# Swapping neighbours in a hand-held order table: four score or value products, two copies and two normalizations in the front of an attention and gated-convolution kernel

## The chip, the cores and the metric

The kernel runs on one core of one Trainium2 chip. The metric is device time in microseconds (us); lower is better.

## The reference

```python
# q, k, v: (8 batches, 12 heads, 448 positions, 64)
scores = scale * np.matmul(q, k.transpose(0, 1, 3, 2))
m = np.max(scores, axis=-1, keepdims=True)
e = np.exp(scores - m)
attn = e / (np.sum(e, axis=-1, keepdims=True) + np.exp(-m) + 1e-09)
x = np.matmul(attn, v)            # then (8, 448, 768)
proj = x @ w_proj                 # (768, 2304), split in x1, x2, x3
X2 = np.fft.rfft(x2, n=S, axis=1)
H = np.fft.rfft(filter_fft, n=S, axis=0)[None, :, :]
x2_conv = np.fft.irfft(X2 * H, n=S, axis=1)
out = (x1 * x2_conv * x3) @ w_out
```

Everything comes in and goes out in float32.

## The kernel before

**Attention** works on pairs of heads; `i` counts them through the whole program (six pairs to a batch, 48 in all, counted from 0, so the seventh pair is 6 and the twelfth is 11). For a pair TensorE first transposes q and k, task T(i), lines 557, 559 and 566, and VectorE copies the result out of PSUM (lines 587 and 576). Then come four score products: S(i,1), S(i,2), S(i,3) (line 866, two matmuls each, one per head, each on 64 rows of the array) and S(i,0), the last 64 keys of both heads together (line 868, one matmul on 128 rows). ScalarE takes the exponential of each, exp(i,t) (lines 879 and 885). ER(i) (line 897, eight matmuls on 64 rows) and V(i,0), V(i,1) (line 905, twelve matmuls each on 128 rows) are the products with the values. The exponentials of pairs 2 and 5 lie in the space of `wout_bf`, which is loaded later, so their rows carry that name. norm(i) on VectorE (lines 918, 919, 920) adds one to the sums that the products carry along, takes the reciprocal and multiplies; only then are the two PSUM banks of V(i) free. X(i) (line 981, copy at line 990) transposes the result.

**The dense part** of a batch b follows its six pairs: folds (lines 1042 to 1050), projections P (1073) and G (1196, with a cast on ScalarE at 1210 and a product on VectorE at 1212), the spectrum Z (1148, casts at 1156, filter products at 1162 and sums at 1168 on VectorE), the inverse I (1243, casts at 1252, halves 1261 and 1263, unfolding 1272, gate 1287), the output O (1009, copies at 1318). Batch 0 also makes the tables and the filter's spectrum (mirror product `rps`, line 771, and `hps`, lines 818 and 821).

**The order** of all this is written out. `Plan` takes 2135 tasks by `add`; each has an engine, needs, makes and takes rings or PSUM banks. `plan.ORDER` (line 432) holds one number for each task: on every engine the tasks stand sorted by that number, and each engine runs its own list strictly in order. `Plan.run` walks the lists once with assumed durations, and in this walk it does two things that depend on the order. It gives each product its bank or pair of banks (eight in all), the one free longest in the walk; a product then waits on the chip for the readers of what lay in that bank before. And it puts **fillers** (matmuls on zeros into a free bank, line 1479) ahead of a TensorE task wherever the walk has TensorE wait there between 8 and 44 us:

```python
                count = int(self.FILL[2] * (at - end) / 0.056)
                ...
                if count >= 2 and free:
                    full[n] = (min(free)[1], count)
```

Fillers are part of the program: they run for their whole length whether TensorE would wait there or not.

Of the kernel before, what the change touches and what calls it, by code (L numbers as in the profile page):

```python
# [314 lines left out]
def kernel(  # L315
# [104 lines left out]
    def stage(g, at, n):  # L420
# [4 lines left out]
    plan = Plan(  # L425
        {
            "e": 6, "er": 2, "e3": 3, "er3": 1, "k0": 2, "q0": 2, "u": 1, "w": 1, "xf": 1,
            "x2": 1, "x2s": 1, "x2b": 2, "xs": 2, "t0": 2, "t1": 2, "yh": 1, "g": 1, "x1": 2, "cr": 2, "cw": 1, "cv": 2, "yT": 1, "yR": 1,
            "os": 3,
        }  # L430
    )
# [1106 lines left out]
    with (  # L1538
# [6 lines left out]
        for b in range(n_batches):  # L1545
            W["yT", b], W["yR", b // 2] = y, yr
            stable(b)
            plan = Plan(plan.size)
# [9 lines left out]
    with tc.manual_schedule(engines={E.PE, E.Pool, E.DVE, E.Activation, E.SP}):  # L1558
        plan = main
# [31 lines left out]
```

## Time and profile before

| | |
|---|---|
| median of the runs | 371.6 us (3 runs, 370.54 to 371.95) |
| the profiled execution | 370.99 us |
| its span, first to last instruction | 369.2 us, mean granted TensorE clock 0.999 |
| TensorE busy (matmul) | 361.6 us, 98% |
| VectorE busy | 258.3 us, 70% |
| ScalarE busy | 263.0 us, 71% |
| GpSimd busy | 112.6 us, 30% |

Read it stage by stage. TensorE is the engine that is busy nearly all the time; the page's slices show its small idle shares at the beginning, near 45 us, near 75 us and at the end. In the timeline a row gives the start, the time from the first start to the last end, the engine, the line, the tiles and the number of instructions; a matmul's end is modelled, so starts are compared with starts. The rows of TensorE give the rows and columns of the array that a matmul uses (64*128 or 128*128).

### The profile page before, as it was taken

The numbers are of one execution on the slowest core, as the hardware profiler recorded it, in microseconds if no ns is written. First come the engines' busy times: TensorE is split into PE (matmuls) and PEld (weight loads), VectorE is DVE, ScalarE is ACT, GpSimd is POOL, SyncE is SP. The second block draws the span as 40 slices with busy tenths as digits, with TensorE's granted clock in tenths as the row PEclk, the third lists the DMA queues.
The fourth block names the chain that finished last, engine by engine and source line by source line (L and its number), as shares of the span: only waits on it lengthen the run. The fifth ranks groups of instructions, "written<-read, shape, count | busy, mean of one in ns | idle before, by whom it ended". The sixth has DMA issues, their size and how long they took to land. (4 is left out here: it accounts for less than half of the span.)

```text
span 369.2 us, 9353 instructions
## 1 busy us (share of the span) xinstructions
PE 361.6 (98%) x3613; PEld 217.1 (59%) x3613; DVE 258.3 (70%) x671; ACT 263.0 (71%) x453; POOL 112.6 (30%) x247
## 2 busy tenths in 40 slices
PE   8999999999999999999999999999999999999995
PEld 6766665656664675654555555665556556555653
DVE  5569388967699648883796868773577845968570
ACT  6889686787777778687688468877778586545623
POOL 7862732344524455414125430411300000000000
PEclk9999999999999999999999999999999999999999
DMA  8999999797998999689999999799855064243125
GB/s 207 273 242 227 255 228 228 174 203 198 183 274 211 221 271 251 181 196 215 259 222 249 229 218 175 224 239 180 197 113 124 2 88 130 42 103 71 43 91 172
DMA packets 132019, 68.41 MB, mean 185 GB/s; under 512 B 88765, under 2 KB 128384, under 8 KB 131968
## 3 DMA queue, kind: packets, MB, share of 16 engines
q1 hardware_dynamic: 127248, 62.11, 74.0%
q0 software_dynamic: 4480, 5.41, 8.4%
q8 instruction: 29, 0.48, 0.6%
q10 hardware_dynamic: 240, 0.23, 0.3%
q14 instruction: 22, 0.18, 0.2%
HBM read 43.86 MB, written 11.01 MB: 149 GB/s over the span
## 5 line engine op out<-in xcount | busy, mean ns | idle before, releaser
L879 ACT ACTIVATE e<-psum 128x896 bf16<-128x896 f32 x138 | 122.2, 922 | 29.9 <-PE psum L866 27.9
L1196 PE MATMUL psum<-xT,wproj_bf 128*128 128x448 bf16 x576 | 121.2, 352 | 0.0
L1196 PEld LDWEIGHTS <-wproj_bf 128*128 128x128 bf16 x576 | 53.9, 98 | 45.6 <-issue 2.2
L1009 PE MATMUL psum<-wout_bf,yT 128*128 128x384 bf16 x288 | 53.1, 326 | 0.0
L663 POOL CAST nat<-nat 112x512 bf16<-112x512 f32 x36 | 23.7, 664 | 88.0 <-DMA nat<-in_q_dram 77.6
L905 PEld LDWEIGHTS <-e 128*128 128x128 bf16 x1104 | 40.5, 98 | 9.8 <-issue 5.8
L905 PE MATMUL psum<-vn,e 128*128 128x65 bf16 x1104 | 46.2, 194 | 0.0
L866 PE MATMUL psum<-qT,kT 64*128 64x448 bf16 x288 | 43.6, 358 | 2.1 <-DVE xb L920 1.4
L1162 DVE TENSOR_TENSOR t<-xs,hrs 113x768 bf16<-113x768 bf16 (+1 forms) x64 | 35.8, 588 | 7.2 <-ACT xs L1156 7.1
L1156 ACT CAST xs<-psum 112x384 bf16<-112x384 f32 (+1 forms) x64 | 29.2, 484 | 15.5 <-PE psum L1144 10.9
L1009 PEld LDWEIGHTS <-yT 128*128 128x128 bf16 x288 | 27.1, 98 | 18.7 <-issue 1.1
L1095 PE MATMUL psum<-xf,wproj_bf 128*128 128x452 bf16 x180 | 38.1, 356 | 0.0
L1318 ACT COPY osb<-psum 128x384 f32<-128x384 f32 x56 | 26.1, 485 | 14.6 <-PE psum L1009 9.3
L920 DVE TENSOR_TENSOR xb<-psum,den 128x512 bf16<-128x512 f32 x48 | 33.2, 691 | 1.7
L1212 DVE TENSOR_TENSOR g<-x,psum 128x448 bf16<-128x448 bf16 x42 | 25.9, 617 | 10.0 <-PE psum L1196 8.0
L885 ACT ACTIVATE er<-psum 128x448 bf16<-128x448 f32 x46 | 25.5, 554 | 8.1 <-PE psum L868 7.9
L1210 ACT CAST x<-psum 128x448 bf16<-128x448 f32 x42 | 22.4, 540 | 10.5 <-PE psum L1196 8.4
L1252 ACT CAST cr<-psum 128x452 bf16<-128x452 f32 x48 | 24.1, 551 | 6.3 <-PE psum L1243 6.3
L918 DVE TENSOR_SCALAR den<-psum 128x8 f32<-128x8 f32 x48 | 7.9, 164 | 28.3 <-PE psum L905 21.5
L695 POOL CAST vn<-nat 128x192 bf16<-128x192 f32 x58 | 23.1, 427 | 14.5 <-DMA nat<-in_v_dram 14.3
L1095 PEld LDWEIGHTS <-wproj_bf 128*128 128x128 bf16 x180 | 16.4, 96 | 17.1 <-issue 1.7
L1073 PE MATMUL psum<-wproj_bf,xf 128*113 128x384 bf16 x144 | 26.4, 327 | 0.0
(136 smaller groups left out, 484.7 us busy)
## 6 DMA issues: line engine op xcount, KB each, us to landing
nat<-in_q_dram SPq DMA_DIRECT2D x47, 224.0 KB, 4.3
out_dram<-osb SPq DMA_DIRECT2D x24, 384.0 KB, 3.8
nat<-in_k_dram SPq DMA_DIRECT2D x41, 192.0 KB, 4.6
nat<-in_v_dram SPq DMA_DIRECT2D x41, 192.0 KB, 4.4
wproj_bf<-in_moe_w_proj_dram POOLq DMA_DIRECT2D x2, 1152.0 KB, 12.3
rests<-in_k_dram SPq DMA_DIRECT2D x8, 192.0 KB, 4.8
rests<-in_v_dram SPq DMA_DIRECT2D x8, 192.0 KB, 3.9
out_dram<-osb SPq DMA_DIRECT2D x8, 192.0 KB, 3.9
```

Of the source, the lines that this page charges most:

```text
L866: nc.tensor.matmul(sc[:, u, 0:S], kT[b % 2][c, hp, t, :], qT[b % 2][c, hp, :])
L879: nc.scalar.activation(to, of, AF.Exp, scale=SCALE)
L905: nc.tensor.matmul(out_bank(u)[:, n, :], P["e"][1 + t][:, u * S + n * 128 : u * S + n * 128 + 128], vn[b % 2][:, hp, 4 * u + t, :], start= ...
L920: nc.vector.tensor_tensor(W["xb", b][:, hp].rearrange("p n (u d) -> p u n d", u=2), op[:, :, :, 0:DH], rec[:].unsqueeze(3).to_broadcast([1 ...
L1009: nc.tensor.matmul(ops[:n, :DCH], y[:, dt, 0:n], wout_bf[:, dt, ch * DCH : (ch + 1) * DCH], start=(dt == 0), stop=(dt == NDT - 1),)
L1073: nc.tensor.matmul(pps[:FQ, :DCH], W["xf", b][:, pg, kt, 0:FQ], wproj_bf[:, kt, D + ch * DCH : D + (ch + 1) * DCH], start=(kt == 0), stop= ...
L1095: nc.tensor.matmul(pps, wproj_bf[:, kt, D + dt * 128 : D + (dt + 1) * 128], W["xf", b][:, :, kt, 0:FQ], start=(kt == 0), stop=(kt == NDT - 1),
L1156: nc.scalar.copy(L["xs", par, ch][:K, pg % 2, :], L["Z", pg, ch][:K, :DCH])
L1162: nc.vector.tensor_tensor(t[:K], L["xs", par, ch][:K], h, op=ALU.mult)
L1196: nc.tensor.matmul(p[:, :S], wproj_bf[:, kt, 2 * part * D + dt * 128 : 2 * part * D + (dt + 1) * 128], xT()[:, kt, 0:S], start=(kt == 0), ...
L1212: nc.vector.tensor_tensor(g[:, dt, :], L["x1", dt], p[:, :S], op=ALU.mult)
L1318: nc.scalar.copy(L["os", st][:n, ch * DCH : (ch + 1) * DCH], L["O", st, ch][:n, :DCH])
```

## The change

One line differs, the table of 2135 numbers, in 37 of them. Most of the 37 are renumberings that follow from a task taking a neighbour's place. One place of the table, as an example (S(2,0) and V(0,1) swap the numbers 20 and 19, and the VectorE copies of T(4) and X(0) swap theirs):

```diff
-    plan.ORDER = (
...
-        40, 28, 6, 14, 31,
...
-        18, 19, 19, 26, 21,
...
+    plan.ORDER = (
...
+        42, 28, 6, 12, 31,
...
+        18, 20, 19, 26, 23,
...
```

What it moves, engine by engine:

- TensorE: S(2,0) goes ahead of V(0,1); V(2,0) ahead of S(4,2); ER(3) and S(4,3) ahead of X(1) and the mirror product; S(5,2) ahead of V(3,0) and S(5,0); V(6,1) five places up, ahead of T(10), three Z and S(8,0); S(12,0) three places up, ahead of three pieces of O.
- VectorE: the two copies of the table `bt` go ahead of the copies of T(1); the copy of X(0) goes behind the copies of T(4); norm(6) goes ahead of the copies of T(10); norm(11) ahead of an unfolding and a gate product.
- ScalarE: exp(13,0) goes ahead of two copies of O.
- GpSimd and SyncE issue the same tasks in the same order; no DMA is moved.

Since banks and fillers come out of the walk, they change too: 86 fillers stand in the program in place of 69, and most products after the first move lie in other banks. In the stretch from T(5) to the first `hps` there were 11, 2, 11 and 3 fillers (ahead of T(5), ER(2), S(4,2) and S(5,3)); now there are 9, 2, 21, 8 and 4 (ahead of T(5), ER(2), ER(3), X(3) and the first `hps`).

TensorE from S(4,0) on, matmuls alone, each run of equal rows written once. Before: S(4,0), 11 fillers, S(4,2), V(2), X(1), the mirror product, ER(3), then S(4,3) and S(5,1) in one run, V(3):

```order
L868 MATMUL psum<-qT_91,kT_89 128x448
L1479 MATMUL psum<-idle 128x128
L866 MATMUL psum<-qT_91,kT_89 128x448
L905 MATMUL psum<-vn_93,wout_bf 128x65
L981 MATMUL psum<-ident_bf,xb 128x128
L771 MATMUL psum<-ft,jm 113x452
L897 MATMUL psum<-vn_93,er_102 128x65
```

Now, in the same words, up to ER(3), with S(4,3), X(1) and the mirror product behind it:

```order
L868 MATMUL psum<-qT_91,kT_89 128x448
L905 MATMUL psum<-vn_93,wout_bf 128x65
L866 MATMUL psum<-qT_91,kT_89 128x448
L905 MATMUL psum<-vn_93,wout_bf 128x65
L1479 MATMUL psum<-idle 128x128
L897 MATMUL psum<-vn_93,er_102 128x65
L866 MATMUL psum<-qT_91,kT_89 128x448
L981 MATMUL psum<-ident_bf,xb 128x128
L771 MATMUL psum<-ft,jm 113x452
L866 MATMUL psum<-qT_91,kT_89 128x448
```

V(2,0) has taken the place of the 11 fillers, a run of 21 fillers has come in ahead of ER(3), and X(1) with the mirror product now parts S(4,3) from S(5,1).

VectorE around norm(6), the difference, from the copies of T(9) on (qT_92 and kT_90 are the transposed q and k of batch 1):

```order
-L587 COPY qT_92<-psum 128x448 x2
-L576 COPY kT_90<-psum 128x512
+L587 COPY qT_92<-psum 128x448
 L918 TENSOR_SCALAR den_108<-psum 128x8
 L919 RECIPROCAL den_108<-den_108 128x8
 L920 TENSOR_TENSOR xb<-psum,den_108 128x2x4x64
```

The two copies of T(10) stood ahead of norm(6) and stand behind it now.

VectorE around norm(11), the difference, in the inverse of batch 0:

```order
 L1263 TENSOR_TENSOR cw<-cr 128x4x111
-L1272 TENSOR_TENSOR cv<-cw 128x2x224
-L1212 TENSOR_TENSOR g<-g,psum 128x448
 L918 TENSOR_SCALAR den_108<-psum 128x8
 L919 RECIPROCAL den_108<-den_108 128x8
 L920 TENSOR_TENSOR xb<-psum,den_108 128x2x4x64
+L1272 TENSOR_TENSOR cv<-cw 128x2x224
+L1212 TENSOR_TENSOR g<-g,psum 128x448
```

norm(11) has passed one unfolding and the gate product that frees the bank of the last G.

More of the change, by code (lines that the diff above doesn't have):

```diff
@@ new lines @@
+    plan.ORDER = (2, 0, 1, 174, 3, 4, 0, 0, 2, 1, 3, 4, 2, 10, 11, 0, 1, 6, 0, 5, 6, 9, 9, 9, 4, 14, 7, 11, 2, 1, 7, 8, 2, 5, 3, 6, 10, 15, 8, 13, 14, 7, 12, 4, 7, 15, 21, 14, 15, 16, 8, 13, 5, 8, 18, 23, 15, 17, 18, 11, 17, 13, 18, 20, 29, 28, 21, 22, 12, 19, 16, 20, 21, 30, 32, 24, 25, 27, 25, 38, 14, 26, 19, 17, 27, 24, 25, 34, 49, 30, 29, 33, 42, 22, 32, 23, 31, 71, 55, 54, 34, 44, 24, 33, 26, 35, 81, 58, 57, 35, 45, 29, 39, 28, 37, 87, 60, 59, 36, 47, 31, 40, 32, 41, 92, 62, 63, 38, 50, 30, 49, 37, 48, 115, 76, 75, 41, 47, 56, 52, 64, 39, 51, 45, 40, 54, 48, 42, 53, 43, 55, 51, 44, 57, 53, 54, 59, 52, 58, 58, 50, 60, 61, 49, 61, 57, 63, 63, 55, 62, 66, 56, 67, 60, 66, 70, 65, 68, 73, 77, 77, 62, 65, 78, 64, 70, 75, 68, 69, 67, 80, 76, 78, 80, 74, 73, 90, 69, 72, 88, 71, 71, 72, 74, 82, 81, 76, 75, 85, 82, 79, 79, 83, 83, 92, 84, 104, 87, 85, 105, 89, 90, 91, 89, 95, 86, 86, 87, 98, 91, 96, 88, 99, 94, 106, 84, 101, 99, 92, 107, 98, 125, 103, 93, 122, 102, 96, 108, 102, 100, 97, 101, 95, 112, 109, 110, 104, 111, 103, 117, 106, 133, 113, 105, 128, 109, 100, 130, 115, 119, 107, 118, 111, 127, 112, 124, 110, 120, 108, 116, 141, 113, 118, 126, 138, 120, 156, 115, 119, 144, 132, 117, 140, 123, 131, 116, 139, 122, 142, 124, 126, 114, 135, 125, 145, 133, 177, 143, 127, 168, 136, 121, 151, 134, 150, 132, 147, 131, 160, 136, 154, 130, 148, 128, 165, 157, 141, 144, 157, 163, 139, 194, 152, 129, 179, 161, 138, 170, 143, 158, 142, 159, 140, 176, 145, 164, 135, 162, 137, 181, 151, 205, 173, 149, 183, 174, 148, 182, 155, 175, 146, 172, 150, 187, 163, 171, 147, 198, 164, 178, 192, 152, 153, 176, 193, 158, 221, 184, 156, 209, 188, 161, 201, 165, 189, 160, 185, 154, 213, 172, 204, 167, 191, 159, 214, 171, 224, 200, 166, 210, 197, 170, 216, 175, 195, 162, 208, 168, 222, 177, 203, 169, 211, 173, 74, 28, 36, 16, 22, 43, 46, 3, 10, 42, 28, 6, 12, 31, 30, 63, 36, 62, 35, 69, 41, 56, 32, 53, 31, 74, 53, 70, 43, 68, 42, 9, 8, 3, 5, 4, 6, 5, 7, 18, 20, 19, 26, 23, 13, 11, 10, 9, 11, 17, 10, 12, 12, 23, 25, 20, 41, 27, 19, 14, 16, 13, 21, 22, 15, 24, 16, 36, 38, 26, 51, 33, 31, 20, 27, 17, 29, 34, 18, 30, 19, 46, 44, 29, 50, 32, 35, 22, 33, 21, 37, 39, 23, 40, 24, 54, 55, 34, 65, 38, 47, 28, 43, 25, 45, 52, 26, 48, 27, 58, 60, 59, 35, 42, 66, 39, 57, 33, 61, 34, 64, 37, 67, 40, 90, 91, 61, 86, 55, 82, 52, 83, 50, 89, 88, 56, 101, 103, 67, 94, 57, 99, 63, 100, 98, 62, 106, 65, 117, 116, 78, 46, 102, 64, 107, 66, 108, 67, 113, 114, 68, 127, 130, 87, 112, 71, 124, 74, 128, 123, 75, 132, 79, 144, 143, 99, 129, 76, 133, 77, 140, 83, 142, 141, 85, 151, 154, 109, 140, 59, 161, 97, 152, 90, 153, 150, 89, 157, 91, 172, 171, 119, 159, 92, 158, 96, 168, 102, 169, 170, 101, 178, 177, 128, 179, 104, 175, 103, 176, 174, 107, 187, 112, 194, 195, 135, 81, 183, 109, 188, 113, 191, 114, 192, 193, 116, 204, 202, 139, 206, 122, 199, 119, 201, 200, 120, 212, 129, 223, 221, 159, 211, 130, 213, 126, 218, 133, 220, 219, 132, 232, 229, 172, 188, 97, 247, 148, 236, 142, 237, 228, 144, 240, 145, 256, 257, 187, 245, 153, 241, 146, 242, 147, 254, 253, 154, 264, 262, 191, 269, 162, 255, 155, 259, 261, 158, 260, 159, 274, 283, 200, 123, 277, 168, 267, 160, 268, 165, 272, 273, 164, 291, 296, 209, 282, 169, 285, 174, 286, 287, 173, 299, 182, 311, 312, 225, 294, 179, 300, 183, 307, 190, 308, 309, 195, 320, 321, 234, 265, 134, 314, 194, 317, 196, 319, 318, 198, 326, 201, 334, 336, 246, 330, 204, 327, 202, 331, 207, 333, 332, 205, 342, 345, 253, 335, 206, 339, 212, 341, 340, 209, 347, 213, 357, 358, 258, 153, 344, 210, 348, 216, 353, 217, 354, 352, 218, 376, 371, 272, 365, 225, 369, 228, 370, 368, 227, 374, 230, 392, 390, 284, 373, 229, 375, 231, 388, 241, 389, 387, 242, 400, 401, 288, 329, 169, 391, 240, 398, 245, 399, 397, 246, 406, 252, 424, 423, 313, 411, 257, 407, 253, 408, 254, 416, 415, 258, 430, 429, 316, 417, 259, 426, 266, 428, 427, 265, 433, 269, 445, 442, 325, 190, 432, 268, 434, 267, 439, 274, 440, 441, 272, 459, 458, 334, 447, 280, 454, 283, 463, 455, 287, 464, 288, 480, 482, 352, 468, 289, 465, 290, 477, 298, 479, 478, 299, 490, 492, 358, 379, 206, 484, 301, 487, 304, 488, 489, 305, 496, 312, 509, 508, 373, 491, 307, 497, 311, 498, 313, 501, 502, 317, 515, 516, 377, 505, 314, 512, 320, 514, 513, 319, 520, 325, 528, 530, 383, 220, 531, 330, 521, 326, 522, 327, 526, 525, 328, 539, 535, 385, 543, 337, 527, 331, 534, 533, 332, 549, 344, 558, 559, 399, 540, 335, 550, 345, 555, 348, 556, 557, 349, 567, 565, 408, 409, 223, 560, 351, 562, 353, 563, 564, 352, 570, 356, 582, 584, 422, 568, 354, 571, 358, 572, 360, 579, 580, 363, 593, 592, 433, 581, 364, 589, 370, 590, 591, 371, 598, 373, 607, 606, 443, 227, 596, 372, 599, 374, 602, 380, 604, 603, 379, 614, 615, 444, 605, 378, 611, 382, 612, 613, 383, 620, 389, 629, 630, 451, 619, 385, 621, 388, 625, 390, 626, 627, 392, 632, 636, 635, 453, 470, 231, 36, 39, 41, 37, 40, 38, 43, 45, 47, 44, 48, 46, 49, 56, 51, 50, 52, 53, 84, 51, 80, 49, 79, 48, 85, 54, 110, 73, 109, 71, 104, 68, 105, 72, 95, 59, 97, 61, 64, 80, 69, 86, 118, 70, 111, 69, 81, 91, 79, 85, 72, 73, 44, 121, 122, 83, 96, 58, 93, 60, 70, 77, 65, 66, 75, 76, 45, 125, 73, 119, 72, 84, 89, 88, 90, 120, 126, 82, 77, 46, 137, 81, 135, 93, 136, 80, 95, 94, 96, 97, 98, 100, 78, 47, 146, 84, 131, 92, 138, 82, 101, 102, 103, 105, 107, 118, 134, 78, 148, 87, 139, 104, 145, 88, 106, 108, 110, 112, 113, 125, 147, 86, 149, 111, 160, 166, 98, 155, 163, 94, 94, 156, 162, 93, 167, 100, 93, 165, 99, 164, 95, 121, 114, 116, 117, 115, 124, 122, 120, 121, 123, 126, 127, 132, 181, 106, 173, 129, 180, 105, 189, 134, 182, 108, 184, 130, 190, 117, 186, 110, 185, 111, 131, 133, 136, 137, 198, 138, 196, 115, 203, 121, 143, 147, 142, 144, 197, 118, 207, 141, 209, 125, 205, 123, 146, 148, 145, 151, 208, 124, 210, 127, 214, 128, 155, 156, 152, 154, 216, 150, 215, 131, 226, 135, 222, 157, 224, 134, 160, 161, 162, 163, 164, 170, 227, 136, 231, 137, 217, 166, 225, 139, 167, 168, 169, 171, 173, 189, 233, 140, 230, 138, 239, 179, 234, 141, 176, 175, 178, 177, 180, 184, 235, 143, 238, 174, 243, 249, 151, 246, 248, 149, 114, 244, 250, 150, 251, 152, 129, 298, 184, 302, 186, 149, 297, 181, 303, 187, 137, 149, 153, 181, 158, 165, 185, 182, 186, 183, 190, 193, 196, 252, 157, 265, 192, 258, 156, 266, 194, 270, 163, 271, 195, 284, 172, 263, 161, 276, 166, 197, 205, 203, 208, 275, 198, 280, 170, 278, 167, 201, 207, 202, 204, 279, 171, 281, 199, 289, 176, 290, 175, 212, 214, 206, 211, 292, 177, 295, 180, 293, 178, 210, 216, 213, 215, 288, 219, 301, 185, 305, 189, 315, 230, 304, 188, 222, 223, 226, 224, 227, 239, 306, 191, 313, 193, 316, 235, 310, 192, 228, 232, 233, 237, 238, 259, 322, 197, 323, 199, 324, 236, 325, 200, 240, 241, 243, 242, 245, 254, 328, 203, 329, 244, 338, 343, 211, 381, 382, 238, 167, 385, 386, 239, 384, 237, 166, 396, 247, 413, 263, 196, 217, 229, 221, 218, 231, 220, 247, 248, 252, 249, 250, 251, 349, 215, 350, 255, 346, 214, 146, 337, 208, 360, 260, 355, 256, 359, 220, 356, 257, 155, 351, 219, 363, 223, 366, 224, 266, 267, 269, 275, 364, 264, 361, 222, 362, 221, 262, 263, 261, 270, 367, 226, 378, 234, 380, 233, 276, 277, 282, 283, 379, 232, 383, 236, 279, 281, 278, 280, 395, 244, 372, 271, 394, 243, 291, 287, 294, 292, 307, 309, 377, 235, 403, 248, 393, 285, 402, 249, 295, 296, 297, 304, 310, 311, 404, 250, 412, 255, 414, 305, 410, 256, 306, 308, 314, 315, 317, 318, 405, 251, 409, 293, 450, 451, 278, 469, 471, 293, 199, 462, 466, 291, 470, 295, 202, 474, 297, 485, 302, 207, 495, 310, 493, 309, 212, 268, 290, 286, 273, 274, 289, 298, 303, 301, 299, 300, 302, 422, 264, 421, 312, 420, 260, 180, 419, 262, 425, 319, 435, 320, 431, 270, 436, 321, 186, 418, 261, 438, 271, 443, 273, 323, 333, 324, 332, 437, 322, 448, 275, 444, 277, 328, 330, 327, 331, 446, 276, 456, 282, 457, 284, 335, 339, 341, 343, 452, 279, 460, 285, 337, 342, 336, 338, 473, 294, 449, 326, 472, 292, 346, 345, 351, 348, 356, 361, 453, 281, 475, 296, 467, 344, 483, 300, 354, 355, 359, 357, 362, 382, 461, 286, 481, 303, 476, 347, 494, 308, 363, 360, 366, 364, 367, 380, 486, 306, 499, 365, 503, 507, 315, 500, 506, 316, 217, 504, 510, 318, 511, 321, 218, 554, 346, 566, 355, 225, 340, 353, 368, 349, 350, 370, 369, 376, 374, 371, 375, 372, 518, 323, 523, 378, 519, 324, 215, 524, 381, 529, 329, 532, 384, 219, 517, 322, 538, 334, 537, 333, 387, 402, 386, 391, 542, 389, 546, 340, 547, 341, 404, 407, 394, 395, 541, 338, 536, 336, 388, 400, 392, 396, 552, 343, 551, 342, 548, 347, 405, 406, 398, 401, 553, 397, 544, 339, 577, 361, 545, 390, 573, 357, 415, 421, 426, 425, 436, 437, 561, 350, 585, 365, 569, 410, 578, 362, 428, 427, 429, 431, 438, 445, 574, 359, 576, 368, 575, 412, 588, 369, 439, 434, 440, 441, 442, 446, 586, 366, 587, 430, 608, 609, 381, 616, 618, 386, 229, 610, 617, 384, 624, 391, 230, 622, 387, 641, 399, 233, 649, 406, 637, 396, 235, 393, 413, 403, 411, 414, 416, 417, 419, 418, 420, 424, 423, 595, 376, 594, 432, 600, 375, 226, 597, 435, 601, 377, 623, 447, 228, 583, 367, 634, 394, 633, 395, 454, 458, 455, 463, 631, 456, 643, 401, 647, 403, 473, 482, 481, 484, 640, 398, 628, 393, 459, 472, 460, 480, 638, 397, 639, 400, 644, 402, 476, 479, 474, 478, 642, 461, 646, 404, 657, 409, 659, 489, 656, 410, 487, 488, 490, 491, 493, 496, 648, 405, 662, 414, 645, 475, 661, 413, 492, 494, 498, 497, 499, 513, 669, 420, 667, 418, 671, 507, 658, 411, 500, 505, 508, 510, 511, 514, 663, 416, 666, 495, 682, 683, 431, 677, 681, 428, 236, 686, 687, 433, 691, 438, 238, 688, 432, 693, 437, 237, 448, 462, 450, 449, 457, 452, 464, 468, 469, 465, 467, 466, 650, 407, 652, 483, 653, 408, 232, 655, 486, 660, 412, 654, 485, 234, 674, 425, 664, 415, 668, 417, 501, 504, 503, 509, 679, 517, 675, 424, 673, 422, 521, 523, 512, 518, 670, 419, 665, 421, 502, 519, 506, 516, 672, 423, 678, 426, 680, 427, 520, 525, 522, 524, 676, 515, 684, 429, 690, 435, 696, 536, 689, 434, 527, 526, 528, 529, 533, 539, 685, 430, 692, 436, 697, 534, 694, 439, 531, 530, 532, 535, 540, 546, 699, 442, 695, 440, 701, 541, 698, 441, 538, 537, 544, 542, 545, 547, 700, 443, 702, 543, 704, 708, 444, 705, 707, 445, 239, 703, 706, 446, 711, 449, 241, 709, 447, 710, 448, 240, 712, 450, 713, 451, 242, 1, 471, 651, 477)
```

1 line of the change is left out of this document (removed).

## The prediction

> **What bounds the kernel now.** First the page's head and busy times, then who waited for whom on TensorE, then the busy time by stretches.
>
> ```profile
> span 369.2 us, 9353 instructions
> PE 361.6 (98%) x3613; PEld 217.1 (59%) x3613; DVE 258.3 (70%) x671; ACT 263.0 (71%) x453; POOL 112.6 (30%) x247
> ```
>
> ```profile
> PE psum L866 <- DVE xb L920: 1.4, 3, 0.6
> PE psum L1487 <- DVE idle L1475: 1.1, 1, 1.1
> PE psum L866 <- DVE kT L578: 0.7, 1, 0.7
> ```
>
> ```profile
> 50.00:60.00 10.00, 10.00 (x109) 6.62 (x106) 8.76 (x22) 6.66 (x11) 0.94 (x2) 1.00 1.15 223
> 70.00:80.00 10.00, 9.40 (x85) 5.27 (x83) 9.45 (x23) 7.17 (x13) 4.44 (x8) 1.00 0.89 194
> 100.00:200.00 100.00, 99.96 (x998) 58.10 (x997) 74.67 (x186) 76.03 (x131) 38.36 (x79) 1.00 0.98 228
> ```
>
> TensorE is the bound: 98% of the span, and 99.96 of 100 us (the first figure behind the length) once the front is over. So what the front has won or lost at 80 us is carried to the end; there is no slack behind it that could swallow either. The change moves no task behind 80 us, though the banks there are dealt anew. ScalarE with 71% and VectorE with 70% are not the bound over the whole, but VectorE comes near it in two stretches, 8.76 and 9.45 of 10 us. Of TensorE's named waits the largest is exactly one kind: a score product (line 866) waiting three times for a normalization (line 920), 1.4 us in all. Those three are S(5,1) behind norm(2), S(8,2) behind norm(6), S(13,1) behind norm(11), and each of these normalizations comes earlier now. The most that can be won is the time lost at these places; the question is what takes it back.
>
> **The change part by part.** I work in starts, since ends of matmuls are modelled. Two unit prices first.
>
> ```profile
> 44.43 0.35 PE L868 MATMUL psum<-qT,kT 128*128 128x448 bf16 x1
> 44.62 0.22 PE L557 MATMUL psum<-ident_bf,ks 128*128 128x128 bf16 x1
> 81.45 0.55 PE L866 MATMUL psum<-qT,kT 64*128 64x448 bf16 x4
> 81.83 0.28 PE L897 MATMUL psum<-vn,er 64*128 64x65 bf16 x8
> ```
>
> A line-868 product followed by another on 128 rows costs 0.19 from start to start. Two line-866 products (four matmuls) followed by others on 64 rows cost 0.38, so 0.19 each.
>
> *Place A, 20 to 28 us.*
>
> ```profile
> 21.09 0.78 PE L1479 MATMUL psum<-idle 128*128 128x128 bf16 x11
> 21.80 0.36 PE L866 MATMUL psum<-qT,kT 64*128 64x448 bf16 x2
> 23.37 0.29 PE L897 MATMUL psum<-vn,er 64*128 64x65 bf16 x8
> 23.50 0.35 PE L866 MATMUL psum<-qT,kT 64*128 64x448 bf16 x2
> 24.31 0.37 PE L866 MATMUL psum<-qT,kT 64*128 64x448 bf16 x2 [0.46 <-DVE xb L920]
> 25.38 0.35 PE L868 MATMUL psum<-qT,kT 128*128 128x448 bf16 x1
> 25.67 0.36 PE L866 MATMUL psum<-qT,kT 64*128 64x448 bf16 x2
> 27.51 0.30 PE L897 MATMUL psum<-vn,er 64*128 64x65 bf16 x8
> 27.91 0.32 PE L818 MATMUL psum<-uw,ft 113*112 113x384 bf16 x1
> ```
>
> ```profile
> 22.20 0.92 ACT L879 ACTIVATE e<-psum 128x896 bf16<-128x896 f32 x1
> ```
>
> Going from 128 rows to 64 costs extra: 25.38 to 25.67 is 0.29 for a product that costs 0.19 above, so 0.10 for a switch. The Trainium skill, "TensorEngine Tiling", section "Tiling Modes" (Key Properties), says that a change of the tiling mode, other than a change of the tile alone, drains the engine. It names no price, and it speaks against this change, which parts runs of 64-row products; were it not so here, the sum would be 0.20 lower. By the two rows at 25.38 and 25.67 the trace agrees with it. Counting the switches from T(5) to the first hps along the order, fillers included (128 rows): 14 before, 16 now, since X(1) parts S(4,3) from S(5,1) and V(3,0) parts S(5,2) from S(5,3), while two fillers' excursions go. That is +0.20.
>
> Fillers: 11 from 21.09 to 21.80, with one switch, are 0.61, so 0.056 each. There were 27 in this stretch and there are 44: +17 × 0.056 = +0.95.
>
> Gone: S(4,3) to S(5,1) takes 0.81 in place of 0.19, −0.62, since S(5,1) now lies in the banks of S(4,2), whose exponential is over at 23.12 even without its earlier start (the ScalarE row at 22.20). ER(4) to hps takes 0.40 where ER costs 0.13 (23.37 to 23.50) and the switch 0.10: −0.17, its place now filled. A wait is added too: X(1) now lies in a bank of norm(2), and behind it on TensorE stand the mirror product, S(5,1) and V(3). But V(2,0) starts where the 11 fillers stood, 0.6 earlier, and 21 fillers of 1.18, ER(3) and S(4,3) of 0.13 and 0.19 and a switch pass between V(2,1) and X(1): 1.6, against the 1.04 of a normalization (the VectorE rows of place C). So this wait is covered; if it is not, it costs at most the 0.46 that S(5,1) waited. Sum of A: 0.95 + 0.20 − 0.62 − 0.17 = **+0.36**.
>
> *Place B, 46 to 61 us.*
>
> ```profile
> 46.53 0.35 PE L868 MATMUL psum<-qT,kT 128*128 128x448 bf16 x1
> 47.17 0.54 PE L905 MATMUL psum<-vn,e 128*128 128x65 bf16 x12
> 47.55 0.35 PE L1148 MATMUL psum<-x,ft 113*113 113x384 bf16 x1
> 48.01 0.61 PE L866 MATMUL psum<-qT,kT 64*128 64x448 bf16 x2
> 48.93 0.37 PE L866 MATMUL psum<-qT,kT 64*128 64x448 bf16 x2 [0.31 <-DVE xb L920]
> 55.14 0.35 PE L868 MATMUL psum<-qT,kT 128*128 128x448 bf16 x1
> 60.91 0.37 PE L866 MATMUL psum<-qT,kT 64*128 64x448 bf16 x2
> ```
>
> ```profile
> 46.92 0.54 ACT L885 ACTIVATE er<-psum 128x448 bf16<-128x448 f32 x1
> 47.36 1.62 ACT L1156 CAST xs<-psum 112x384 bf16<-112x384 f32 x4
> 60.57 1.15 DVE L1212 TENSOR_TENSOR g<-g,psum 128x448 bf16<-128x448 bf16 x2 [0.56 <-PE psum L1196]
> ```
>
> S(8,1) to S(8,2) takes 0.92, of which 0.73 is lost. Only a part returns. V(6,1), 0.38 long (47.17 to 47.55), now stands ahead of S(8,0), which starts at 46.91 in place of 46.53. Its exponential follows 0.39 later (47.30), the four casts of Z 0.44 after that (47.74), and S(8,2) now lies in a bank that the second cast frees: the casts are 0.38 apart and 0.48 long ((1.62 − 0.48) / 3), so it is free at 48.60, and S(8,2) starts about 48.65: **−0.28**, not −0.73. The copies of T(10) are now a normalization later, and who waits for them are pair 10's scores, which start at 55.14: some 7 us of cover, without which they would cost the 1.04 of norm(6). Later, other banks: S(10,2) now lies where the first of two gate products reads (60.57, two in 1.15, so over at about 61.18); it starts at 61.23 in place of 60.91: **+0.32**. For S(9,2) and S(10,0), which change banks as well, I take +0.10 between 0 and that 0.32. Sum of B: **+0.14**.
>
> *Place C, 73 to 80 us.*
>
> ```profile
> 75.14 0.36 PE L866 MATMUL psum<-qT,kT 64*128 64x448 bf16 x2
> 76.11 0.37 PE L866 MATMUL psum<-qT,kT 64*128 64x448 bf16 x2 [0.60 <-DVE xb L920]
> 76.61 2.44 PE L1009 MATMUL psum<-wout_bf,yT 128*128 128x384 bf16 x14
> ```
>
> ```profile
> 73.37 1.73 ACT L879 ACTIVATE e<-psum 128x896 bf16<-128x896 f32 x2 [1.05 <-PE psum L866]
> 74.09 0.39 DVE L1272 TENSOR_TENSOR cv<-cw 128x448 bf16<-128x448 bf16 x1
> 74.40 0.61 DVE L1212 TENSOR_TENSOR g<-g,psum 128x448 bf16<-128x448 bf16 x1
> 74.93 0.16 DVE L918 TENSOR_SCALAR den<-psum 128x8 f32<-128x8 f32 x1
> 75.97 0.38 DVE L1272 TENSOR_TENSOR cv<-cw 128x448 bf16<-128x448 bf16 x1
> ```
>
> S(12,3) to S(13,1) takes 0.97, so 0.78 is lost; S(13,1) now lies in the banks of S(12,1), whose exponential, the first of the two at 73.37, is over before 75. But the gate product moves behind norm(11): norm(11) takes 1.04 (74.93 to 75.97), starts near 74.05, then unfolding 0.31 (74.09 to 74.40) and the gate product 0.61 end at 76.01, and the first piece of O lies in the bank that it frees: 76.06 in place of 76.61: **−0.55**. S(12,0) costs 0.19 here and is missing two pieces of O later: nothing. Its exponential and those of pair 13 come up to 1 us earlier, which no TensorE task of this place waits for.
>
> *The rest at nothing:* S(2,0) ahead of V(0,1), both 128 rows; the copies of bt, X(0) and exp(13,0), since the copies that they pass are followed on TensorE by fillers or by products that read other tiles. If that cover is gone each costs one operation of its engine, by the VectorE rows above 0.39 to 0.61; if the passing copy was the one waited for, the same is gained. I take 0, and the ends go into the range. No DMA moves.
>
> Sum: 0.36 + 0.14 − 0.55 = **−0.05 us** on a profiled span of 369.2 (with the profile's 1.8 around it, 370.99). The median of the runs is 371.6, so **371.5**. Half a per cent, 1.86 us, is about what a measurement of this kernel can tell from no change; the sum is far below it.
>
> **The rivals.**
> *The waits go and nothing grows in their place:* −0.62 − 0.17 − 0.73 − 0.78, with the fillers and switches of A (+1.15): −1.15, 370.5. For it: the three waits are real and all three causes move earlier. Against it: the rows of B and C, which show the next wait close behind.
> *The fillers cost and the waits only change names:* A without its gain (+1.15) and B with +0.42 and no gain: +1.57, 373.2. For it: the walk that places fillers and banks knows no chip time.
> *VectorE falls behind:* it is 8.76 and 9.45 busy of 10 us in the two stretches above. A normalization of 1.04 put ahead of copies that free banks can hold TensorE by its whole length, twice: +2.08, with A +2.44, 374.0. It decides once the copies of T(10) or the gate products end after TensorE reaches their bank. Against it: VectorE still waits for TensorE before the gate products (0.56 at 60.57).
> *All four waits go and the fillers lie where TensorE would wait anyway:* −2.30, 369.3; the 0.46 in the row at 24.31 stood behind only 11 fillers, so little speaks for it.
>
> **How the numbers follow.** The forecast has 0.58, the clean gain 0.20, the filler case 0.10, VectorE behind 0.08, the full gain 0.04. The range takes in the clean gain and the filler case: 370.4 to 373.2. Faster by over half a per cent is the full gain alone, 0.04; slower VectorE behind, 0.08; within it the rest, 0.88.
>
> **What would show it.** In the profile after: no wait of line 866 for line 920 at the three places; 21 fillers ahead of ER(3), about 1.2 us; TensorE waiting at a Z or S(8,2) for ScalarE near 47 us, for line 1212 near 61 and near 76 us. Matched starts should lie +0.4 at 28 us, +0.1 at 50, +0.5 at 62 and 0.0 from 80 us on. A shift that grows behind 80 us, or a wait of over 1 us for VectorE in 50 to 70 us, makes the prediction wrong.

## The result, and the profile after

| | before | changed |
|---|---|---|
| median of the runs | 371.08 us (370.41 to 372.31, 9 runs) | 372.03 us (371.50 to 372.69, 9 runs) |
| the profiled execution, its span | 370.99 us, 369.2 us | 372.44 us, 370.7 us |

The ratio is 1.0025, 95% interval [1.0013, 1.0037]: the changed kernel is about 0.9 us slower, where no change was forecast. A second set of its runs (below) gave 1.0046 [1.0030, 1.0063]. These intervals must be read with one more number: the kernel before, run in the changed kernel's place, came out at 1.0019 [1.0001, 1.0036] against itself, with a median of 371.38 us. So about 0.4 us between "this" and "before" says nothing, and below I compare every kernel with those 371.38 us as well. The sets of runs come from several chips; the kernel before has medians of 371.08, 371.07, 370.88 and 370.96 us in them. The median of all 15 runs of the changed kernel lies 0.87 us above that (resampling the runs, as I did it, gives [0.31, 1.34]).

The time lies in the forecast's range, but a change of about nothing was forecast and a loss was measured. The page's head and the waits on TensorE of the changed kernel:

```profile
span 370.7 us, 9391 instructions
PE 361.8 (98%) x3630; PEld 217.1 (59%) x3630; DVE 257.5 (69%) x671; ACT 263.0 (71%) x453; POOL 113.7 (31%) x247
```

```profile
PE psum L1487 <- DVE idle L1475: 1.1, 1, 1.1
PE psum L1144 <- DMA x<-nat: 0.7, 1, 0.7
PE psum L866 <- DVE kT L578: 0.7, 1, 0.7
PE psum L566 <- POOL ldm L524: 0.4, 1, 0.4
PE psum L1009 <- DVE yT L1287: 0.3, 1, 0.3
PE psum L866 <- DVE g L1212: 0.3, 1, 0.3
PE psum L1148 <- ACT er L885: 0.3, 1, 0.3
```

The 1.4 us in which score products waited for a normalization are gone. In their place stand five new waits of 0.3 us or more (in all, times, longest), and the largest is for a kind of work that the prediction never names: a DMA transpose (line 1112) that a spectrum product (line 1144) reads, 190 us behind the last task that was moved.

Where the time went, by the starts of the same tasks in two traces, subtracted (changed, or an experiment, minus before; each column is the growth of that difference). The column "at 20 us" is what the start of the program happened to bring in that execution.

| kernel | at 20 us | place A, 20 to 28 | place B, 28 to 65 | place C, 72 to 83 | behind 83 us | median, and against 371.38 |
|---|---|---|---|---|---|---|
| changed | −0.42 | +0.49 | +0.41 | −0.38 | +1.33 | 372.03, +0.65 |
| changed, second set | −1.32 | +0.49 | +1.16 | −0.43 | +0.94 | 372.54, +1.16 |
| place A alone | −0.25 | +0.49 | +0.50 | +0.04 | +1.10 | 372.22, +0.84 |
| place B alone | −0.26 | 0.00 | +1.02 | 0.00 | +0.17 | 371.75, +0.37 |
| place C alone | −0.48 | +0.01 | −0.06 | −0.01 | +1.59 | 371.20, −0.18 |
| ER(3), S(4,3) alone | +1.15 | +0.95 | −0.06 | −0.41 | +2.27 | 372.78, +1.40 |
| V(2,0) and place C | −0.84 | −0.24 | −0.06 | −0.12 | +0.91 | 371.23, −0.15 |
| changed, fewer fillers | −0.56 | +0.14 | +0.83 | −0.33 | +2.49 | 372.51, +1.13 |
| changed without ER(3), S(4,3) and S(5,2) | −0.74 | −0.40 | +0.57 | −0.28 | +1.35 | 371.38, 0.00 |
| before again | +0.02 | 0.00 | −0.06 | 0.00 | −0.07 | 371.38 |
| changed, transposes earlier | −0.22 | +0.49 | +0.84 | +0.03 | +1.56 | 371.89, +0.51 |
| before, transposes earlier | −0.82 | 0.00 | −0.05 | +0.24 | +1.13 | 371.73, +0.35 |
| V(2,0), C, transposes earlier | +0.15 | −0.24 | −0.06 | −0.48 | +1.34 | 372.08, +0.70 |

Three things are to be seen. Place A repeats to 0.01 us wherever the whole of it is in. The column behind 83 us, where no task of the attention's front is moved, is positive for every altered kernel and about zero for the kernel before: that is the part of the account which the prediction had at nothing. But each row is one execution, and some lie far from the median of their kernel: place C alone 372.13 us (median 371.20), ER(3) and S(4,3) alone 374.98 (372.78), the changed kernel with the transposes earlier 373.72 (371.89). So a single figure of that column is not what a kernel costs; the medians tell that.

In the changed kernel's column behind 83 us two places make up nearly all. 0.40 is lost near 120 us, at a piece of O that waits for the gate on VectorE (line 1287), and 0.88 near 270 us, at Z(5,0,1), which waits for a DMA transpose. In its second trace the first is gone (−0.10) and the second is there again (+0.96).

### The profile page after: what moved, and what is told of

Its sections match the earlier page's. It is cut to its first block, busy times and chain, and to the rows that moved or that the text cites. A ratio compares the mean times of both kernels' runs of the same rounds, so it can differ in the third digit from the quotient of the medians.

```text
span 370.7 us, 9391 instructions
## 1 busy us (share of the span) xinstructions
PE 361.8 (98%) x3630; PEld 217.1 (59%) x3630; DVE 257.5 (69%) x671; ACT 263.0 (71%) x453; POOL 113.7 (31%) x247
## 5 line engine op out<-in xcount | busy, mean ns | idle before, releaser
L663 POOL CAST nat<-nat 112x512 bf16<-112x512 f32 x36 | 24.6, 689 | 88.5 <-DMA nat<-in_q_dram 73.9
L866 PE MATMUL psum<-qT,kT 64*128 64x448 bf16 x288 | 42.7, 354 | 1.1 <-DVE kT L578 0.7
```

Of the source, the lines that this page charges most:

```text
L866: nc.tensor.matmul(sc[:, u, 0:S], kT[b % 2][c, hp, t, :], qT[b % 2][c, hp, :])
```

## The experiments

Each edit is a replacement of numbers in the order table, written as a map from a task's place in the table to its new number. The first three kernels have it in two lines of their own, so that their source lines lie two further down (line 866 is 868 there).

**The three places one by one, and the changed kernel again.**

```diff
     plan.ORDER = (...)
+    at = {454: 20, 472: 19, 39: 13, 40: 14, 426: 12, 66: 21, 67: 22, 457: 23,
+          481: 36, 504: 37, 423: 42, 470: 41, 505: 39, 507: 40, 495: 46, 514: 47, 518: 45}
+    plan.ORDER = tuple(at.get(i, n) for i, n in enumerate(plan.ORDER))
```

> Only the moves of place A (before 30 us) are made. Theory front-sum (what the changed kernel lost is lost where its tasks moved, place by place, and carried to the end): TensorE's starts lie +0.5 us later from 28 us on, measured against their own offset at the 19 first fillers, with 44 fillers in the stretch and 16 switches, and nothing is given back, so +0.5 us in the time. Rival late-chance (the front is about zero, and the time goes into waits behind 100 us that come and go): time as before within 0.3 us, unless a wait of 0.3 us or more shows behind 100 us.

Place B alone and place C alone:

```diff
+    at = {124: 92, 539: 91, 553: 94, 1089: 95, 1111: 96, 1113: 93, 125: 62, 126: 63, 540: 61}
```

> Only the moves of place B (V(6,1), norm(6)) are made. Front-sum: starts -0.3 us at 50 us, then +0.2 to +0.4 at 62 us, because S(10,2) is given the bank that the gate product at 61 us frees; +0.2 to +0.4 in the time. Rival late-chance: same as before within 0.3 us. A third way, that the gain at S(8,2) lasts: -0.3 us.

```diff
+    at = {601: 109, 1171: 110, 1178: 111, 604: 161, 1183: 163, 1187: 162, 1194: 164,
+          617: 92, 1184: 94, 1188: 93}
```

> Only the moves of place C (norm(11), S(12,0), exp(13,0)) are made. Front-sum: starts -0.4 to -0.5 us from 80 us on, and the time 0.4 to 0.5 us below before. Rival late-chance: the gain does not reach the end, since TensorE waits for other things behind 100 us: time as before within 0.2 us.

The changed kernel again, without an edit:

> The changed kernel once more, for a second trace. Front-sum: +0.5 us at 80 us against the offset at the first fillers; the two waits behind 100 us of the first trace (0.40 at the O product near 120 us, 0.88 at the Z product near 270 us) come back only if something in the order makes them. Late-chance: at least one of them is gone or has another size, and the time differs from the first trace's by that much.

Ratios: A 1.0026 [1.0007, 1.0046], B 1.0023 [1.0007, 1.0039], C 1.0007 [0.9987, 1.0026], changed again 1.0046 [1.0030, 1.0063]. C brings nothing in time, and the places do not simply add. A and B are slower than the kernel before they ran against, but hardly more so than that kernel against itself (1.0019); against 371.38 us, resampling gives A +0.84 [−0.04, 1.89] and B +0.37 [−0.33, 0.98], so a cost of either alone is likely and not shown. Of the forecasts at the front, place A's +0.5 came, but +0.50 more came in place B, where nothing was moved; place B brought +1.02 for +0.2 to +0.4, and place C −0.01 for −0.4 to −0.5. Two walls show why a gain can be lost. In the timeline of the changed kernel, norm(7) on VectorE (the row of line 920 below) ends near 52.08 and the run of six matmuls from 52.02 holds S(8,3), S(9,1) and S(9,2):

```profile
52.02 0.95 PE L866 MATMUL psum<-qT,kT 64*128 64x448 bf16 x6
49.46 1.18 DVE L1162 TENSOR_TENSOR t<-xs,hrs 113x768 bf16<-113x768 bf16 x2 [0.88 <-ACT xs L1156]
51.39 0.69 DVE L920 TENSOR_TENSOR xb<-psum,den 128x512 bf16<-128x512 f32 x1
```

In the second trace of the same kernel TensorE comes 0.9 us earlier; the same rows there, and the GpSimd casts beside them:

```profile
51.99 0.83 PE L866 MATMUL psum<-qT,kT 64*128 64x448 bf16 x4 [0.52 <-DVE xb L920]
48.55 1.93 DVE L1162 TENSOR_TENSOR t<-xs,hrs 113x768 bf16<-113x768 bf16 x2 [0.87 <-ACT xs L1156]
51.25 0.69 DVE L920 TENSOR_TENSOR xb<-psum,den 128x512 bf16<-128x512 f32 x1
48.84 0.61 POOL L524 CAST ldm<-nat 112x512 bf16<-112x512 f32 x1
49.40 1.29 POOL L531 CAST vn<-nat 128x192 bf16<-128x192 f32 x2
```

The two filter products start 0.91 earlier, but take 1.93 in place of 1.18, since they now begin beside the GpSimd cast of line 524, which the first trace has at 48.92 to 49.54, all but ahead of them; norm(7) ends 0.14 earlier, not 0.9, and S(9,1), which lies in the banks that it frees, waits 0.52. The Trainium skill, "Trainium Architecture — The Big Picture", section "What this means for kernel authors", says that VectorE and GpSimd share a port pair by an exclusive lock; by the 1.93 against 1.18 the trace agrees, and so does the kernel before, where 0.39 us of that cast fall into the products and they took 1.72. So 0.52 us of TensorE's lead is given back there in this trace. It is no fixed wall: with V(2,0) and place C (below) TensorE is 1.1 us early, the products take 1.33 us, norm(7) is early too and S(9,1) does not wait. The second wall is S(13,1) near 75.5. With place C alone norm(11) is early, yet:

```profile
75.57 0.36 PE L868 MATMUL psum<-qT,kT 64*128 64x448 bf16 x2 [0.59 <-DVE cv L1274]
```

The releaser named, an unfolding, writes nothing that this product reads. What it reads last is the transpose of k of its own pair, kT(13): issued at 71.09, and the list of DMA issues in 70 to 72 us, first of the kernel before and then of place C alone, gives its time to landing:

```profile
kT<-nat SPq DMA_TRANSPOSE x1, 2.8
kT<-nat SPq DMA_TRANSPOSE x1, 4.4
```

It lands at 75.53. In the kernel before, where S(13,1) waited for norm(11) until 76.11, it had landed at 73.22 and nobody saw it. The order need not differ for this: the kernel before with two later transposes moved (below) has the same program up to there, and its kT(13) took 4.8 us.

**Which part of A.**

ER(3) and S(4,3) alone, on the kernel before:

```diff
-    add = plan.add
+    at = {423: 42, 470: 41, 505: 39, 507: 40}
+    plan.ORDER = tuple(at.get(i, n) for i, n in enumerate(plan.ORDER)); add = plan.add
```

> Of place A only ER(3) and S(4,3) are put ahead of X(1) and the mirror product (rps); all else stands as before. Theory 'the order of place A costs': these two were cover for X(1)'s wait, and the programme of the fillers answers with 90 in place of 69; the front loses 0.6 to 0.9 us from 28 us on, and the time is 0.5 to 1.0 us above before (ratio 1.0015 to 1.003). Rival 'late-chance' (what the front loses is lost in the late waits for transposes and VectorE, whatever was moved): the front moves under 0.3 us, and the time is above before only by late steps, 0 to 0.6 us.

V(2,0) and place C, on the kernel before:

```diff
+    at = {481: 36, 504: 37, 601: 109, 1171: 110, 1178: 111, 604: 161, 1183: 163,
+          1187: 162, 1194: 164, 617: 92, 1184: 94, 1188: 93}
```

> V(2,0) ahead of S(4,2), and all of place C; the rest of A and all of B left as before. Theory 'front-sum': V(2,0) brings 0.25 us at 28 us and place C 0.4 to 0.5 at 80 us, so starts lie 0.5 to 0.7 us earlier from 80 us on and the time is 0.4 to 0.7 us under before (ratio 0.998 to 0.999). Rival 'walls': norm(7) ending near 52.1 us and the transposes of pair 13 landing near 75.5 us hold TensorE wherever it comes from, so the gain at 28 us is gone at 53 us and that of C at 76 us; the starts behind 80 us lie within 0.2 us of before and the time within 0.3 us.

In the changed kernel, one line ahead of `add = plan.add` (the programme of fillers ran to 44.0 before):

```diff
+    plan.FILL = (8.0, 20.0, 0.9)
```

> The changed kernel with no filler planned behind 20 us: 35 fillers fewer. Theory 'fillers cost what they last': at 0.056 us each they take up to 2.0 us; TensorE waits in place of some of them (X(1) for norm(2), X(3), hps), so place A comes out at about -0.1 to 0.2 in place of +0.49, and the time is 0.2 to 0.5 us under the changed kernel's. Rival 'fillers lie where TensorE would wait anyway': the starts at 28 us stay at +0.4 to +0.5, waits for VectorE stand where fillers stood, and the time is the changed kernel's within 0.2 us. A third way, the clock: without fillers the granted clock falls under 1.00 behind 20 us and the time rises by over 0.5 us.

The changed kernel's numbers but for ER(3), S(4,3), X(1), the mirror product, S(5,0), V(3,0) and S(5,2):

```diff
+    at = {454: 20, 472: 19, 39: 13, 40: 14, 426: 12, 66: 21, 67: 22, 457: 23, 481: 36, 504: 37,
...
+          617: 92, 1184: 94, 1188: 93}
```

> The changed kernel without two parts of place A: ER(3) and S(4,3) stand behind X(1) and the mirror product as before, and S(5,0), V(3,0), S(5,2) in the order of before. V(2,0), S(2,0), the copies, B and C are as changed. Theory 'front-sum': A falls from +0.49 to about -0.4, B keeps what it brings or costs (0.0 to +0.4), C brings -0.4; from 80 us on the starts lie 0.4 to 0.6 us ahead of before and the time 0.2 to 0.6 us under before. Rival 'walls': what place A brings is lost at S(9,1) behind norm(7) (wait of 0.5 us or more) and at S(13,1) behind the transposes; the time is that of before or up to 0.6 us above it.

Ratios: ER(3) and S(4,3) alone 1.0043 [1.0026, 1.0061]; V(2,0) and C 1.0010 [0.9997, 1.0023]; fewer fillers 1.0035 [1.0020, 1.0051]; without the back of A 1.0007 [0.9994, 1.0021]. So the part that costs is narrowed down: four numbers of the 37 alone cost as much as the whole change (+1.40 us against 371.38, by resampling [0.23, 2.14]), and the changed kernel without them and without S(5,2) takes the time of before, 0.87 us under the 15 runs of the changed kernel ([0.32, 1.45]). (S(5,2) was not tried alone.) Alone the four bring 21 fillers more into the stretch up to the first hps: 10 ahead of ER(3), 7 ahead of S(5,1), 7 ahead of ER(4), and 3 fewer ahead of S(5,3). At 0.056 each that is 1.18; place A grows by 0.95. But the fillers are only the form of the loss. The changed kernel with its 21 fillers ahead of ER(3), and then the one without them:

```profile
21.82 1.33 PE L1479 MATMUL psum<-idle 128*128 128x128 bf16 x21
23.09 0.30 PE L897 MATMUL psum<-vn,er 64*128 64x65 bf16 x8
23.51 0.40 PE L981 MATMUL psum<-ident_bf,xb 128*128 128x128 bf16 x4
22.53 0.69 DVE L920 TENSOR_TENSOR xb<-psum,den 128x512 bf16<-128x512 f32 x1
```

```profile
21.77 0.29 PE L897 MATMUL psum<-vn,er 64*128 64x65 bf16 x8
21.91 0.35 PE L866 MATMUL psum<-qT,kT 64*128 64x448 bf16 x2
23.14 0.38 PE L981 MATMUL psum<-ident_bf,xb 128*128 128x128 bf16 x4 [0.88 <-DVE xb L920]
```

ER(3) could start at 21.77, as soon as V(2) is out; the order in which it stands then leaves X(1) waiting 0.88 for norm(2), whose bank X(1) took. Before, X(1) and the mirror product lay elsewhere, started while V(2) ended and norm(2) began (22.86 to 23.37), and ER(3) and S(4,3) followed them. The move took the cover away from norm(2), and the walk laid fillers on the hole. Taking them out makes place A +0.14 in place of +0.49, but the time stays where it was (372.51 us, against 372.03 and 372.54): in its trace S(9,1) waits 0.20, and 2.49 is lost behind 83 us. The theory has place A right and the time wrong. The clock is not the reason: without the fillers it was granted at 1.00 from 20 to 60 us as well.

V(2,0) gains on the front as expected (−0.24), and norm(7) does not take it back; C's gain is held by the transpose of pair 13 (−0.12 is left). In time the two gain nothing. In their trace S(15,0) loses 0.7 us at once:

```profile
88.15 0.36 PE L868 MATMUL psum<-qT,kT 128*128 128x448 bf16 x1 [0.55 <-DMA kT<-nat]
```

Without the back of A the same two places wait, less than the rival said: S(9,1) 0.19 us for norm(7), S(13,1) 0.33 for its transpose.

**The late loss.** In three kernels two transposes move up SP's queue: the one of Z(3,0,1) ahead of two loads and X(24), the one of Z(5,0,1) ahead of the second of two stores. This was done to the changed kernel, to before, and to V(2,0) with C (there kT(13) and kT(15) pass one and two loads as well). With them ran the kernel before, unchanged, for a second trace.

> The kernel before, unchanged, for a second trace. Theory 'landing gates': TensorE is held at a few late products by the landing of DMA transposes on the one queue of SP, whichever kernel runs; in a second trace Z(3,0,1) near 186 us and Z(5,0,1) near 269 us start within 0.2 us of a landing again, and if TensorE comes there earlier than in the first trace it waits by that much. Rival 'late loss comes with the change': TensorE again meets these two without a wait of 0.2 us or more, wherever it comes from. The ratio is 1 within its interval.

The changed kernel with the two transposes earlier:

```diff
+    at = {1495: 152, 332: 153, 790: 154, 320: 155, 1756: 218, 1725: 219}
```

> The changed kernel with two DMA transposes put earlier on SP's queue, nothing else: the one that Z(3,0,1) reads ahead of two loads and the transpose X(24), the one that Z(5,0,1) reads ahead of the second of two stores. Theory 'landing gates': they land 1 to 3 us earlier, the waits of 0.3 to 1.1 us at Z(3,0,1) and Z(5,0,1) are gone, and the time is 0.5 to 1.0 us under the changed kernel's, which leaves +0.0 to +0.5 of the loss against before (what the front loses). Rival 'the queue is the bound': the same wait comes back at a later transpose or store, since the queue carries as much as before; the time is the changed kernel's within 0.3 us.

The same edit on the kernel before:

> The kernel before with the same two transposes put earlier on SP's queue. Theory 'landing gates': in its trace TensorE came to both products just as the transposes landed, so its own gain is smaller: 0.0 to 0.5 us under before (ratio 0.9985 to 1.000). Rival 'the queue is the bound': 0.0, or a later wait and up to 0.3 us above.

```diff
+    at = {481: 36, 504: 37,
...
+          1495: 152, 332: 153, 790: 154, 320: 155, 1756: 218, 1725: 219,
+          154: 52, 157: 53, 170: 64, 184: 65, 176: 66}
```

> V(2,0) ahead of S(4,2) and all of place C, with the two transposes of the two kernels above put earlier, and kT(13) ahead of the load sq(14), kT(15) ahead of the loads sk(17) and sk(16) on SP's queue. Theory 'landing gates': what V(2,0) and C bring (0.25 and 0.4 us) is no longer lost at S(13,1), S(15,0), Z(3,0,1) and Z(5,0,1); the time is 0.5 to 1.0 us under before (ratio 0.997 to 0.9985), the best of all. Rival 'the queue is the bound': the delayed loads hold other products, and the time is that of before within 0.3 us.

Ratios: before again 1.0019 [1.0001, 1.0036], where 1 was forecast; changed 1.0023 [1.0004, 1.0042]; before 1.0024 [1.0003, 1.0045]; V(2,0) with C 1.0027 [1.0004, 1.0050]. None is told from the unchanged kernel's own 1.0019, so no version here is shown to beat the kernel before. Z(5,0,1) in four traces: changed, changed again, before again, and changed with the transposes earlier:

```profile
269.98 0.70 PE L1144 MATMUL psum<-x,ft 113*113 113x384 bf16 x3 [0.72 <-DMA x<-nat]
269.40 0.70 PE L1144 MATMUL psum<-x,ft 113*113 113x384 bf16 x3 [0.80 <-DMA x<-nat]
268.54 0.65 PE L1144 MATMUL psum<-x,ft 113*113 113x384 bf16 x3
271.15 0.65 PE L1144 MATMUL psum<-x,ft 113*113 113x384 bf16 x3
```

In before again its transpose had landed at 268.23, in the first trace at 268.48 with the product starting at 268.60: TensorE comes there 0.1 to 0.3 us behind the landing, with no wait and next to no slack. TensorE came no earlier in the second trace, so that one cannot tell the two theories apart. The second trace of the changed kernel says more: TensorE comes at 268.60 again, and the transpose, issued 0.16 us earlier than in before, lands at 269.36. It is the landing that is late there, not TensorE that is early.

Of the "landing gates" theory the place is right, the cure is not: with the transposes earlier, the transpose of Z(5,0,1) took 4.6 us to land in place of 5.6, its wait is gone, and waits came up elsewhere. From the same kernel's list:

```profile
PE psum L866 <- DMA kT<-nat: 0.9, 2, 0.7
PE psum L566 <- POOL ldm L524: 0.6, 1, 0.6
PE psum L1144 <- DVE g L1212: 0.4, 1, 0.4
```

The kernel before with the transposes earlier is the plainest case. Its front is untouched, its execution began 0.82 us early, and 0.58 of that was gone at 150 us, ahead of the first transfer that was moved, at products that read transposes of k (S(13,1) +0.24, S(15,0) +0.49). At its end it was 0.50 late; of what it lost behind 150 us, 0.72 came near 187 and 194 us, at three products that wait for VectorE (lines 1212 and 920). So being early is not kept, as the rival "the queue is the bound" says, and two of its three times come about right: 371.89 against 372.03, 371.73 against 371.38. The third, 372.08 for V(2,0) with C, is 0.7 above 371.38 and outside both forecasts.

That the queue is the bound is not shown. The edit does more than its text says: SP's order is part of the walk, and the walk deals 115 of the 590 banks and pairs anew, from Z(3,0,1) on. S(30,1), one of the three products near 194 us, has been given the banks of norm(28), for which it now waits. The page's DMA slices, before and changed, do show engines that are busy for most of the span:

```profile
DMA  8999999797998999689999999799855064243125
DMA  8999999789998999898999999796855054243125
```

A digit is the busy share of the 16 DMA engines in a slice, in tenths. They stand at 7 or more (but for one 6) to slice 28, or 258 us, and mostly at 9. But Z(5,0,1) lies behind that. In the changed kernel the share (the number ahead of the last) is 0.42 just before its transpose goes out, and the queue of SP itself waits there for VectorE's copies (line 1106) that the two transposes of this batch read (between 254 and 272 us, 5.4 us in two waits, the longest 3.7):

```profile
258.00:262.00 4.00, 4.00 (x51) 2.15 (x49) 2.11 (x5) 2.57 (x4) 2.29 (x5) 1.00 0.42 80
```

```profile
SPq L1112 <- DVE nat L1106: 5.4, 2, 3.7
```

The Trainium skill, "DMA: Bandwidth & Descriptors", section "Issuing engines are not separate DMA queues", says that transfers of all issuers interleave on the same 16 engines. No run here shows it across issuers. Within SP's own queue the transpose for Z(5,0,1), with one store ahead of it in place of two, took 4.6 us in place of 5.6 in the changed kernel, 4.0 in place of 4.6 in the kernel before, and 4.2 in place of 4.7 with V(2,0) and C.

## Why the prediction was wrong, step by step

**"What the front has won or lost at 80 us is carried to the end; there is no slack behind it."** This is the step that failed. From TensorE's 99.96 of 100 us I read that nothing else could set the end, and put everything behind 80 us at nothing. It was not nothing: the difference grew by 1.33 and 0.94 us behind 83 us, of which 0.88 and 0.96 at Z(5,0,1), whose transpose landed 0.9 to 1.5 us later than before. And a lead is not carried: V(2,0) with C, and the changed kernel without the back of A, come to 83 us with 0.42 and 0.11 won and take the time of before. TensorE comes only 0.1 to 0.3 us behind the landing at Z(5,0,1), so there is no slack, but what stands in the way is another work's end, not TensorE's. Why landings come later is argued and not shown: a front that is late or early changes when transfers start and which of them meet. The rows of 50 to 60, 70 to 80 and 100 to 200 us had a DMA share of 1.15, 0.89 and 0.98 beside TensorE's, and I left that column out. The prediction named a shift that grows behind 80 us as its own refutation.

**The sum up to 80 us, −0.05.** It was off as well. Against 20 us, the matched starts were to lie at +0.4, +0.1, +0.5 and 0.0 at 28, 50, 62 and 80 us; they lay at +0.49, +0.19, +0.90 and +0.52, and in the second trace at +1.22 in the end. That the time still lies in the range says little: the range is 2.8 us wide, and a front mis-sized by 0.5 us and a late loss of about 1 us that was left out both fit into it.

**Place A, +0.36.** Measured +0.49 in four traces: the sign of the sum is right and its size near. "This wait is covered" is not: the cover of 1.6 us for norm(2) was the 21 fillers themselves, 1.27 of it. Without them the wait is 0.88. I counted fillers once as a cost and once as the work that hides a wait; the question for the order was what useful work stands there, and that was 0.3 us.

**Place B, +0.14.** S(8,2) came out at −0.30 (−0.28 forecast) and S(10,2) at +0.32, with the 0.33 for line 1212 near 61 us (+0.32 forecast). The +0.10 for the products that only changed banks was too small: in the first trace S(9,1) and S(9,2) took +0.15 and ER(8) +0.24, which makes B +0.41 in all. And S(9,1) behind norm(7) was not seen as a wall: in the second trace it makes up 0.68 of the +1.16 that the place costs. The waits foretold near 47 us (0.3, line 1148 for ScalarE) and 61 us are there; the one for line 1212 near 76 us didn't show as a wait.

**Place C, −0.55.** −0.38 and −0.43 in the changed kernel, where the transpose of k has landed in time; next to nothing in C alone (−0.01) and in the changed kernel with the transposes earlier (+0.03), where it has not. Where it has, S(13,1) brings the 0.78 of the forecast, and what is missing to −0.55 goes at a piece of O near 77.5 us that waits for the gate (line 1287). The trace of before would have cleared kT(13), which landed there 2.9 us ahead of its product (73.22 to 76.11); that the time to landing itself moves, from 2.8 to 4.4 us, was not reckoned with.

**The rest at nothing.** It was not tested by itself. In the changed kernel without the back of A, V(2,0) accounts for 0.24 of the 0.40 that A then gains; the other 0.16 is not explained by a run.

**The rivals.** VectorE falling behind was put at copies and gate products; what came was a normalization behind filter products, at half the size. "The waits only change names" describes what happened best, though it had the new names among fillers and banks alone, and the largest new one is a transfer.

What stays open: how much of the late loss belongs to the changed order and how much to the executions that were traced, why the transpose for Z(5,0,1) took 5.0 to 5.7 us to land in six of these traces and 4.3 to 4.7 in five (with the same stores ahead of it in all of them), and why the traces of before are so alike (0.07 us at every task looked at) when its runs spread over 2 us.

## What to carry to other kernels

An engine that is busy all the time need not be the only bound: look up, for each product that is to come earlier, when its transfers land, what they queue behind and what they wait for, and count a gain only up to the latest of its releasers. Filler work in front of a wait is no cover; ask what the wait would be without it. Before a quarter of a per cent is believed, run the unchanged kernel against itself.

## What was not expected of the hardware

A DMA transpose on SP's queue took 2.8 us from issue to landing in one place and 4.4 in the same place of another kernel, 0.65 us later, with nothing changed in the queue's order, and 4.8 us in a third whose program is the same as in the first up to there. A pair of filter products on VectorE took 1.18 or 1.93 us by where GpSimd's casts fell. And the start of the program alone, up to 20 us, differs by up to 2.5 us between traces (−1.32 to +1.15 in the table). In the +1.15, ER(3) and S(4,3) alone, the granted clock was 0.90 in 5 to 10 us and 0.76 in 10 to 15 us; in every other trace it was 1.00 there.
